# Strassen's scheme for the second mixture's first product, in pairs of token tiles

## The chip, the cores and the metric

The kernel runs on one core of one Trainium2 chip. Its engines work beside each other, each through its own queue in order: PE multiplies matrices into PSUM, ACT and DVE work on tiles in SBUF and PSUM, POOL on tiles in SBUF, SP's queue issues most DMA transfers. The metric is the device time of one execution in microseconds, as the median of several runs.

## The reference

A memory attention feeds two mixtures. What the change touches is the second one, on 4608 tokens of 512 features:

```python
x = _moe_ref(x=x, **moe_kwargs)                 # 4608 x 512, from the first mixture
h = x @ w_in                                    # w_in 512 x 1024
h_max = np.max(h, axis=-1, keepdims=True)
e = np.exp(h - h_max)
sm = e / (np.sum(e, axis=-1, keepdims=True) + 1e-09)
solu = h * sm
mu = np.mean(solu, axis=-1, keepdims=True)
var = np.mean((solu - mu) ** 2, axis=-1, keepdims=True)
ln = (solu - mu) / np.sqrt(var + 1e-06) * g_ln
return (ln @ w_out).astype(np.float32)          # w_out 1024 x 512
```

## The kernel before

Attention and the first mixture go over eight batches, each in two halves (`n`, `j`). In a half, `gemm1` makes 2048 hidden features in eight pairs `fp` (24 matmuls of 288 columns each; ACT squares, DVE casts and subtracts), and `gemm2` four blocks `d` of the result (48 matmuls each). ACT scales each block, `absmax` takes its maximum on DVE, and SP stores it to DRAM (`x2_d`), in groups of 1152 tokens that share one power-of-two scale.

The second mixture works on 36 tiles of 128 tokens. Every operand of a product is kept as two float16 tiles, a high part (written by ACT) and the rest (a subtraction on DVE): `split`. A product then takes three passes: high by high, high by low, low by high. For tile `i`: `load_x` fetches it, `split_x` splits it, `gemm3` multiplies it with `w_in` (4 blocks of 128 features x 3 passes x 2 halves of 512 columns = 24 matmuls, into two PSUM banks). `solu_1` takes the row maximum out of PSUM (DVE) and Exp (ACT). `solu_2` multiplies the product with Exp and takes mean and variance (DVE), then POOL takes the power -1/2 and normalises. `solu_3` casts to the high half of `nat` (ACT), `solu_4` subtracts for its low half (DVE) and has SP transpose it by DMA to `lt`. `gemm4` multiplies `lt` with `w_out` (8 blocks x 3 passes = 24 matmuls of 512 columns), ACT scales the result, SP stores it.

The order on every engine is the order of the program (a manual schedule). In the last half of batch 7, PE's `gemm2` of blocks 1 to 3 alternates with `gemm3` of tiles 0 to 2; from there on `gemm3` of one tile alternates with `gemm4` of one three tiles back. The weights of the second mixture are split at `prep2`, steps 0 to 3, between blocks of `gemm2`. The maximum of the last group of tokens is taken by a matmul (`mm_max`).

Of the kernel before, what the change touches and what calls it, by code (L numbers as in the profile page):

```python
# [66 lines left out]
def tile_mem_attention__moe_relu2__solu_ln(  # L67
# [15 lines left out]
    nc = tc.nc  # L83
# [14 lines left out]
    NTILE = NT // 128  # L98
    scale = 1.0 / float(D) ** 0.5
# [21 lines left out]
    xsc = const.tile([128, NT // GRP], FP32)  # L121
    xiv = const.tile([128, NT // GRP], FP32)
# [968 lines left out]
    def gemm1(n, j):  # L1091
        if j == 0:
            cs, t = csc_t[n]
            nc.vector.tensor_scalar(out=cs, in0=iw, scalar1=t[:, 0:1], scalar2=None, op0=ALU.mult)
        for fp in range(KF // 2):
            gemm1_mm(n, j, fp)
            relu(j, fp)
            square(j, fp, "A")
            nc.vector.tensor_copy(  # L1099
                out=g_of(n, j, 0)[:, 2 * fp:2 * fp + 2, 0:BLK], in_=gt["r2", j, fp]  # L1100
            )
            square_lo(n, j, fp)
            if fp == 2 and j == 0:
                phi_sum(n + 1)

# [81 lines left out]
    def gemm2_mm(n, j, d, part=(0, 1)):  # L1187
# [5 lines left out]
        half = len(steps) // 2  # L1193
        for x in range(half * part[0], half * (part[-1] + 1)):
# [221 lines left out]
    def prep2_open():  # L1416
        attn_ctx.close()
        for nm, bufs in (("x", 3), ("s", 2), ("o", 2), ("m", 1)):
            pools_b[nm] = ctx.enter_context(tc.tile_pool(name=f"pb_{nm}", bufs=bufs))
        W2["t"] = wts.tile([128, 2, KD * DFF2 + KF2 * DM], FP16, tag="win", name="w2_t")  # L1420
        for i in range(8):
            tag = ("e2", "so", "nat", "lt")[i // 2]
            W2[i] = pools_b["s"].tile([128, 2, 512], FP32, tag=tag, name="w2", bufs=4 if tag == "lt" else 2)
            nc.sync.dma_start(out=flat(W2[i]), in_=w2_d[i])
        pools_b["ones"] = pools_b["m"].tile([128, 128], FP32, tag="ones", name="ones_m")
        nc.gpsimd.memset(pools_b["ones"], 1.0)

    def prep2_scale(nm):
        mx = st.tile([128, 1], FP32, tag="wmx", name="wmx", bufs=1)
        word_value(pk_t.pop(("m", nm)), mx)  # L1430
        if nm == "in":
            wsc = st.tile([128, 1], FP32, tag="w2sc", name="w2sc", bufs=1)
            nc.vector.tensor_copy(out=wsc, in_=pow2_scale(mx, iw2, "wsc"))
# [7 lines left out]
    def prep2_split(i):  # L1441
        nm, x = P2[i]
        if nm == "in":
            dst = W2["t"][:, :, x * DFF2:(x + 1) * DFF2]
            split(dst[:, 0], dst[:, 1], W2[i].rearrange("p a f -> p (a f)"), pk_t["s", nm])
        else:
            for a in range(2):
                kk = 2 * x + a
                dst = W2["t"][:, :, KD * DFF2 + kk * DM:KD * DFF2 + (kk + 1) * DM]
                split(dst[:, 0], dst[:, 1], W2[i][:, a], sgl[:, kk:kk + 1])  # L1450
# [8 lines left out]
    PREP2 = (  # L1459
        ((0, 1), ()), ((2, 3), ()), ((4, 5), ()), ((6, 7), (0,)), ((), (1,)), ((), (2,)), ((), ()), ((), ()),  # L1460
    )

    def prep2(i):
        sp, tiles = PREP2[i]
        if i == 2:
            for x in range(3):
                load_x(x)
        for x in sp:
            prep2_split(x)
        for x in tiles:  # L1470
            split_x(x)
            load_x(x + 3)
# [20 lines left out]
    def x_scale(g):  # L1493
        sc = pow2_scale(xal_t.pop(g), xiv[:, g:g + 1])
        nc.vector.tensor_copy(out=xsc[:, g:g + 1], in_=sc)
        nc.vector.tensor_tensor(out=xiv[:, g:g + 1], in0=xiv[:, g:g + 1], in1=iw2, op=ALU.mult)

    def split_x(i):
        if i >= NTILE:
            return  # L1500
        g = i * 128 // GRP
        if g in xal_t:
            x_scale(g)
        t = xt_t.pop(i)
        xs = pools_b["x"].tile([128, 2, KD, 128], FP16, tag="xs", name="xs")
        split(xs[:, 0], xs[:, 1], t, xsc[:, g:g + 1])
        xs_t[i] = (xs, xiv[:, g:g + 1])

    def gemm3(i):
        xs, iv = xs_t.pop(i)  # L1510
        wt = W2["t"][:, :, 0:KD * DFF2].rearrange("p a (k f) -> p a k f", k=KD)
        hp = ps_h.tile([128, 2, 512], FP32, tag="h", name="hp2")
        for kk in range(KD):
            for px, pws in ((0, (0, 1)), (1, (0,))):
                for pw in pws:
                    for a in range(2):
                        nc.tensor.matmul(  # L1517
                            out=hp[:, a, :],
                            lhsT=xs[:, px, kk, :],
                            rhs=wt[:, pw, kk, a * 512:(a + 1) * 512],  # L1520
                            start=(kk == 0 and px == 0 and pw == 0),
                            stop=(kk == KD - 1 and px == 1),
                        )
        return hp, iv
# [3 lines left out]
    def solu_1(i, hp, iv):  # L1528
        hv = hp.rearrange("p a f -> p (a f)")
        mx = st.tile([128, 1], FP32, tag="hmx", name="hmx")  # L1530
        nc.vector.tensor_reduce(out=mx, in_=hv, op=ALU.max, axis=AX)  # L1531
        nm = st.tile([128, 1], FP32, tag="nm", name="nm")
        nc.vector.tensor_scalar(out=nm, in0=mx, scalar1=iv[:, 0:1], scalar2=-1.0, op0=ALU.mult, op1=ALU.mult)  # L1533
        split_x(i + 3)
        load_x(i + 6)
# [3 lines left out]
            out=e, in_=hv, func=ACTF.Exp, scale=iv[:, 0:1], bias=nm[:, 0:1], accum_out=sm  # L1539
        )  # L1540
        so_t[i] = hv, iv, e, sm

    def solu_2(i):
        hv, iv, e, sm = so_t[i]
# [20 lines left out]
        so_t[i] = so  # L1565

    def solu_3(i):
        so = so_t[i]
        nat = pools_b["s"].tile([128, 2, DFF2], FP16, tag="nat", name="nat")
        nc.scalar.copy(out=nat[:, 0, :], in_=so)  # L1570
        so_t[i] = so, nat

    def solu_4(i):
        so, nat = so_t.pop(i)
        nc.vector.tensor_tensor(out=nat[:, 1, :], in0=so, in1=nat[:, 0, :], op=ALU.subtract)  # L1575
# [4 lines left out]
        ln_t[i] = lt  # L1580
# [12 lines left out]
    def gemm4(i):  # L1593
        lt = ln_t.pop(i)
        wt = W2["t"][:, :, KD * DFF2:].rearrange("p a (k f) -> p a k f", k=KF2)
        y = ps_y.tile([128, 512], FP32, tag="y", name="y2")
        steps = [(f, pl, pw) for f in range(KF2) for pl, pw in PASSES]
        for x, (f, pl, pw) in enumerate(steps):
# [3 lines left out]
                rhs=wt[:, pw, f, :],  # L1602
                start=(x == 0),
                stop=(x == len(steps) - 1),
            )
        o = pools_b["o"].tile([128, DM], FP32, tag="o", name="o")
        nc.scalar.activation(out=o, in_=y[:, 0:DM], func=ACTF.Copy, scale=io2[:, 0:1])  # L1607
        for x, (off, n, bb, c, p) in enumerate(runs(i * 128, 128)):
            eng = nc.scalar if i == NTILE - 1 and x else nc.sync
            eng.dma_start(out=out_v[bb, c, p:p + n, :], in_=o[off:off + n, :])  # L1610

# [50 lines left out]
    with tc.manual_schedule():  # L1662
# [16 lines left out]
        def tile_mm(i):  # L1679
            h3_t[i] = gemm3(i)  # L1680

        def tile_rest(i):


            solu_1(i, *h3_t.pop(i))
            if i:
                solu_3(i - 1)
            if i == NTILE - 1:
                solu_4(i - 1)
            solu_2(i)  # L1690
            if i and i != NTILE - 1:
                solu_4(i - 1)

        h3_t = {}
        LAST = NB - 1
        for n in range(1, NB):
            for j in range(2):
# [7 lines left out]
                for d in range(KD):  # L1705
# [66 lines left out]
```

## Time and profile before

| | us |
|---|---|
| median of 3 runs | 1079.24 |
| lowest and highest | 1078.04, 1079.5 |
| the profiled execution, its time | 1078.8 |
| the profiled execution, its span from first to last instruction | 1077.0 |

The profile is one execution. An engine's busy share is an average over the whole span; the kernel has stages of quite different make-up, so stages are read by stretches of time. In the stage of the second mixture PE alternates between `gemm3` (line 1517) and `gemm4` (line 1599), from 687 us to the end.

### The profile page before, as it was taken

How to read it: one execution, taken by the hardware profiler on the slowest of the kernel's cores; microseconds unless marked ns; L12 is line 12 of the kernel's file. 1: busy time of each engine (PE TensorE's matmuls, PEld its weight loads, DVE VectorE, ACT ScalarE, POOL GpSimd, SP SyncE). 2: the span in 40 equal slices, each digit the busy share in tenths (PEclk: the TensorE clock that was granted, in tenths of full speed). 3: DMA queues.
4: the chain of work that ended last, by engine and by line, in shares of the span. 5: the costliest groups of instructions: out<-in, count | busy, mean ns of one | idle time of the engine just before them, and what ended most of it. 6: DMA issues, size and time to landing. Idle time of an engine off the chain costs nothing.

```text
span 1077.0 us, 21231 instructions
## 1 busy us (share of the span) xinstructions
PE 1053.2 (98%) x8679; PEld 694.4 (64%) x8679; DVE 767.3 (71%) x1469; ACT 525.8 (49%) x775; POOL 174.1 (16%) x157
## 2 busy tenths in 40 slices
PE   5799999999999999999999999999999999999998
PEld 4577777777777777777777777754444444444443
DVE  4799988877777777777776866467666766666662
ACT  3689755663663663563664566332333333333322
POOL 0000200220120120120120100023223232232320
PEclk9999999999999999999999999999999999999999
DMA  9993534734734635635624142124343343443324
GB/s 303 268 269 128 127 109 93 173 90 101 173 91 112 162 91 117 156 92 129 144 91 106 37 175 62 41 73 115 89 115 100 100 108 88 108 106 100 88 59 108
DMA packets 204849, 129.25 MB, mean 120 GB/s; under 512 B 137424, under 2 KB 187856, under 8 KB 204752
## 3 DMA queue, kind: packets, MB, share of 16 engines
q1 hardware_dynamic: 204608, 127.70, 45.4%
q8 instruction: 68, 1.11, 0.5%
q14 instruction: 29, 0.24, 0.1%
q10 hardware_dynamic: 112, 0.20, 0.1%
q0 software_dynamic: 32, 0.00, 0.0%
HBM read 71.83 MB, written 23.07 MB: 88 GB/s over the span
## 4 chain that ended last, share of the span: by engine, by line
PE 96%; DMA 2%; DVE 1%; SPq 0%; issue 0%; ACT 0%; ACTq 0%
PE y L1196 33%; PE y L1599 17%; PE hp L1517 17%; PE hp L1114 15%; PE hp L1010 3%; PE y L1038 3%; DMA q_s<-in_q_dram 2%; PE wp L734 2%; PE sp L883 1%; PE kp L524 1%; PE wp L692 1%; DMA wt_s<-in_v_dram 1%; PE kp L564 1%; PE tq L644 0%; SPq L383 0%; PE kp L538 0%
## 5 line engine op out<-in xcount | busy, mean ns | idle before, releaser
L1196 PE MATMUL y<-g,w_out 128*128 128x288 f16 x2688 | 338.6, 286 | 0.0
L1196 PEld LDWEIGHTS <-w_out 128*128 128x128 f16 x2880 | 277.2, 97 | 86.5 <-issue 12.0
L1517 PE MATMUL hp<-w_t,xs 128*128 128x512 f16 x864 | 192.0, 379 | 0.0
L1599 PE MATMUL y<-w_t,lt 128*128 128x512 f16 x864 | 191.7, 379 | 0.0
L1114 PE MATMUL hp<-aT,vwt 128*128 128x288 f16 x1344 | 166.9, 286 | 0.0
L1114 PEld LDWEIGHTS <-vwt 128*128 128x128 f16 x1344 | 131.4, 98 | 33.2
L1599 PEld LDWEIGHTS <-lt 128*128 128x128 f16 x864 | 84.5, 98 | 101.7
L1517 PEld LDWEIGHTS <-xs 128*128 128x128 f16 x864 | 84.5, 98 | 101.4
L1561 POOL TENSOR_TENSOR rstd<-ve,nhalf 128x1 f32<-128x1 f32 x36 | 52.7, 1464 | 332.6 <-DVE mv L1559 332.6
L1531 DVE TENSOR_REDUCE hmx<-hp 128x1 f32<-128x1024 f32 x36 | 44.1, 1224 | 84.1 <-PE hp L1517 84.1
L322 ACT ACTIVATE xs<-xt,xsc 128x512 f16<-128x512 f32 x36 | 26.0, 721 | 151.3 <-PE hp L1517 129.9
L1213 ACT ACTIVATE x<-y,bcol,cs 128x288 f32<-128x288 f32 x60 | 35.2, 586 | 111.1 <-PE y L1196 96.2
L1179 DVE TENSOR_TENSOR g<-r_s,g 128x576 f16<-128x576 f32 x112 | 85.6, 764 | 3.8
L1172 ACT ACTIVATE r_s<-r 128x576 f32<-128x576 f32 x112 | 76.6, 684 | 17.5 <-DVE g L1179 14.3
L1125 ACT ACTIVATE r<-hp 128x576 f32<-128x576 f32 x120 | 77.5, 646 | 13.9 <-PE hp L1114 6.9
L319 DVE TENSOR_REDUCE xmx<-x 128x1 f32<-128x288 f32 x64 | 28.8, 450 | 53.6 <-ACT x L1213 53.3
L1099 DVE CAST g<-r_s 128x576 f16<-128x576 f32 x112 | 51.7, 462 | 21.3 <-ACT r_s L1172 21.3
L1538 ACT ACTIVATE e<-hp,nm,xiv 128x1024 f32<-128x1024 f32 x36 | 43.3, 1203 | 45.5 <-DVE nm L1533 45.5
L1607 ACT ACTIVATE o<-y,io 128x512 f32<-128x512 f32 x36 | 24.7, 687 | 53.0 <-issue 40.5
L1575 DVE TENSOR_TENSOR nat<-so,nat 128x1024 f16<-128x1024 f32 x36 | 43.8, 1216 | 5.4 <-ACT nat L1570 5.4
L1554 DVE BATCH_NORM_STATS2 bs<-so 128x6 f32<-128x512 f32 x72 | 46.3, 685 | 1.2
L1549 DVE SCALAR_TENSOR_TENSOR so<-hp,sm,e 128x1024 f32<-128x1024 f32 x36 | 46.2, 1284 | 1.3
(256 smaller groups left out, 1187.9 us busy)
## 6 DMA issues: line engine op xcount, KB each, us to landing
x_d<-x SPq DMA_DIRECT2D x64, 144.0 KB, 2.0
xt<-x_d SPq DMA_DIRECT2D x36, 256.0 KB, 3.1
kv_s<-in_k_dram SPq DMA_DIRECT2D x31, 288.0 KB, 8.2
kv_s<-in_v_dram SPq DMA_DIRECT2D x31, 288.0 KB, 8.8
q_s<-in_q_dram SPq DMA_DIRECT2D x21, 288.0 KB, 4.9
out_dram<-o SPq DMA_DIRECT2D x23, 192.0 KB, 2.6
w_out<-in_moe_w_in_dram SPq DMA_DIRECT2D x4, 1024.0 KB, 18.1
raw<-in_moe_w_out_dram SPq DMA_DIRECT2D x4, 1024.0 KB, 11.4
```

What stands on the lines that cost most here:

```text
L1099: nc.vector.tensor_copy(out=g_of(n, j, 0)[:, 2 * fp:2 * fp + 2, 0:BLK], in_=gt["r2", j, fp])
L1114: nc.tensor.matmul(out=hp[:, u, 0:BLK], lhsT=vt[:, pw, R, f * 128:(f + 1) * 128], rhs=aT[:, CJ * j:CJ * (j + 1), pa, R, :], start=(x == 0) ...
L1125: nc.scalar.activation(out=r, in_=gt.pop(("h", j, fp))[:, :, 0:BLK], func=ACTF.Relu, scale=scale)
L1172: nc.scalar.activation(out=r2, in_=r, func=ACTF.Square)
L1179: (nc.vector if eng == "D" else nc.gpsimd).tensor_tensor(out=g_of(n, j, 1)[:, fs, 0:BLK], in0=gt.pop(("r2", j, fp)), in1=g_of(n, j, 0)[:, ...
L1196: nc.tensor.matmul(out=y[:, 0:w], lhsT=w_out_t[d][:, pw, f, :], rhs=g_of(n, j, pg)[:, f, 0:w], start=(x == 0), stop=(x == len(steps) - 1),)
L1517: nc.tensor.matmul(out=hp[:, a, :], lhsT=xs[:, px, kk, :], rhs=wt[:, pw, kk, a * 512:(a + 1) * 512], start=(kk == 0 and px == 0 and pw == ...
L1531: nc.vector.tensor_reduce(out=mx, in_=hv, op=ALU.max, axis=AX)
L1549: nc.vector.scalar_tensor_tensor(out=so, in0=hv, scalar=sm[:, 0:1], in1=e, op0=ALU.mult, op1=ALU.mult)
L1554: nc.vector.bn_stats(out=bs[:, a, :], in_=so[:, a * 512:(a + 1) * 512])
L1561: nc.gpsimd.tensor_tensor(out=rstd, in0=ve, in1=nhalf, op=ALU.pow)
L1599: nc.tensor.matmul(out=y[:, 0:DM], lhsT=lt[:, pl, f, :], rhs=wt[:, pw, f, :], start=(x == 0), stop=(x == len(steps) - 1),)
```

## The change

The product with `w_in` is made for pairs of tiles by the Strassen scheme in Winograd's form. The pair's x is a 2 x 2 array of blocks (two token tiles, two halves of 256 features), `w_in` another (two halves of features, two halves of 512 columns). Eight block products become seven, of sums and differences. The four sums of x blocks are made on POOL (`sums_x`), those of `w_in` once, also on POOL (`w2_sums`). A block product is 6 matmuls of 512 columns. Each pair has three PSUM banks, two sets of them; what was read from PSUM by the steps that follow is now put together in an SBUF tile `so` of float32: ACT copies a bank (four copies to a pair), products are added on in the bank, and DVE adds two more banks to what was copied (`h_add`, three to a pair). Maximum, Exp and `solu_2` then read SBUF.

`pair` writes out the order of one pair's steps together with the rest of the pair before. `gemm4` is cut into quarters of 6 matmuls that stand between the block products (`fill`); in pairs 0 and 1 quarters of `gemm2` of blocks 1 to 3 of the last half take these places. Splits of x go in two parts. `prep2` is laid out anew: steps 5 and 7 stand in `gemm1` of the last half, and the split of `w_out` (`prep2_out`) stands in pair 0. The maximum of the last group is taken by POOL's all-reduce. Scales change by powers of two.

```diff
     def gemm1(n, j):
...
+            if n == NB - 1 and j:
+                prep2(4 + fp)
...
+    def gemm2_q(n, j, d, part):
+        gemm2_mm(n, j, d, (part,), 4)
+        if part == 3:
+            gemm2_out(n, j, d)
...
+    def w2_sums(k):
+        b11, b12 = W2[k][:, 0], W2[k][:, 1]
+        b21, b22 = W2[2 + k][:, 0], W2[2 + k][:, 1]
+        t = [pools_b["x"].tile([128, 2, 512], FP32, tag="xt", name="w2s") for x in range(2)]
+        for out_, x, y in ((t[0][:, 0], b12, b11), (t[0][:, 1], b22, t[0][:, 0]), (t[1][:, 0], b22, b12),
+                           (t[1][:, 1], b21, t[0][:, 1])):
+            nc.gpsimd.tensor_tensor(out=out_, in0=x, in1=y, op=ALU.subtract)
+        W2["sum", k] = t
...
     def prep2(i):
...
+        if i == 0:
+            w2_sums(0)
+            for k in range(2):
+                w2_split(k, 0)
+                w2_split(k, 1)
+        elif i == 1:
+            w2_split(0, 2)
+            w2_split(0, 3)
+            w2_sums(1)
+        elif i == 2:
+            w2_split(1, 2)
+            w2_split(1, 3)
+            load_x(0)
+            load_x(1)
+        elif i == 3:
+            sums_x(0)
+            x_col(0)
+        elif i == 5:
+            split_part(0, 0)
+        elif i == 7:
+            split_part(0, 1)
+            load_x(2)
+            sums_x(1)
...
+    def sums_x(p):
...
+        a11, a12, a21, a22 = x_blocks(p)
+        sm = pools_b["x"].tile([128, 4, 2, 128], FP32, tag="xm", name="xm", bufs=1)
+        for x, in0, in1, op in (
+            (0, a21, a22, ALU.add), (1, sm[:, 0], a11, ALU.subtract),
+            (2, a11, a21, ALU.subtract), (3, a12, sm[:, 1], ALU.subtract),
+        ):
+            nc.gpsimd.tensor_tensor(out=sm[:, x], in0=in0, in1=in1, op=op)
...
+    def split_part(p, part):
...
+        parts = ((slice(3, 7), xt_t["m", p]),) if part == 0 else (
+            (slice(0, 2), t[:, :, 0:128].rearrange("p (b k) t -> p b k t", b=2)),
+             (slice(2, 3), t[:, 2:4, 128:256].unsqueeze(1)),
+        )
+        for b, src in parts:
+            nc.scalar.activation(out=xs[:, 0, b], in_=src, func=ACTF.Copy, scale=sc)
+        for b, src in parts:
+            nc.vector.scalar_tensor_tensor(
+                out=xs[:, 1, b], in0=src, scalar=sc, in1=xs[:, 0, b], op0=ALU.mult, op1=ALU.subtract
+            )
...
+    PROD = {1: (0, 0, 0), 2: (2, 1, 1), 5: (1, 3, 3), 6: (0, 4, 4), 3: (1, 6, 2), 7: (0, 5, 5), 4: (0, 2, 6)}
+
+    def product(p, i):
+        xs = xs_t[p][0]
+        bank, a, b = PROD[i]
+        first = i in (1, 2, 5)
+        steps = [(kk, px, pw) for kk in range(2) for px, pws in ((0, (0, 1)), (1, (0,))) for pw in pws]
+        for x, (kk, px, pw) in enumerate(steps):
+            nc.tensor.matmul(
+                out=hp_t[p][bank],
+                lhsT=xs[:, px, a, kk, :],
+                rhs=W2["lo"][kk][:, b, :] if pw else W2["hi"][:, b, kk, :],
...
+    def h_add(out_, bank):
+        nc.vector.tensor_tensor(out=out_, in0=bank, in1=out_, op=ALU.add)
+
+    def pair(p, fill, at=(2, 1, 1, 3)):
...
+        for i in (1, 2, 5):
+            product(p, i)
+        if p:
+            solu_max(q, 1)
+        split_part(p + 1, 0)
+        out4(2 * p - 5)
+        nc.scalar.copy(out=ha[:, 0:512], in_=bx)
+        if p:
+            solu_exp(q, 1)
+        h_add(ha[:, 0:512], bz)
+        fills(at[0])
+        if p:
+            solu_2(q, 1)
+            solu_3(q, 0)
+        nc.scalar.copy(out=hb[:, 512:1024], in_=by)
+        if p:
+            solu_4(q, 0)
+        split_part(p + 1, 1)
+        load_x(p + 3)
+        if p == 0:
+            for x in range(4):
+                prep2_out(x)
+        product(p, 6)
+        fills(at[1])
+        product(p, 3)
+        nc.scalar.copy(out=ha[:, 512:1024], in_=bx)
+        if p:
+            solu_3(q, 1)
+        sums_x(p + 2)
+        fills(at[2])
+        h_add(ha[:, 512:1024], by)
+        solu_max(p, 0)
+        product(p, 7)
+        out4(2 * p - 4)
+        solu_exp(p, 0)
+        h_add(hb[:, 512:1024], bx)
+        if p:
+            solu_4(q, 1)
+        fills(at[3])
+        solu_2(p, 0)
+        product(p, 4)
+        nc.scalar.copy(out=hb[:, 0:512], in_=bx)
+        fills(8)
...
+        pair(0, [lambda d=d, x=x: gemm2_q(LAST, 1, d, x) for d in (1, 2) for x in range(4)])
+        pair(1, [lambda x=x: gemm2_q(LAST, 1, 3, x) for x in range(4)], (0, 1, 1, 2))
+        x_max(3)
+        xal_t[3] = all_max(xal_t[3], "xal")
+        for p in range(2, NPAIR):
+            pair(p, tiles4(p - 2))
+        p = NPAIR - 1
+        rest = tiles4(p - 1) + tiles4(p)
+        solu_max(p, 1)
+        out4(2 * p - 3)
+        solu_exp(p, 1)
+        solu_2(p, 1)
+        solu_3(p, 0)
+        solu_4(p, 0)
+        for x, f in enumerate(rest):
+            f()
+            if x == 2:
+                solu_3(p, 1)
+                solu_4(p, 1)
```

In `pair`, `q` is the pair before, `ha` and `hb` are the two tiles' rows of `so`, and `bx`, `by`, `bz` the three banks.

## Rows read from the trace of the kernel before

**Rows 1.** The page's table of engines: busy us (share of the span), instructions.

```profile
PE 1053.2 (98%) x8679; PEld 694.4 (64%) x8679; DVE 767.3 (71%) x1469; ACT 525.8 (49%) x775; POOL 174.1 (16%) x157
```

**Rows 2.** Stretches of time: busy us of each engine, PE clock, DMA share, GB/s.

```profile
640.00:690.00 50.00, 50.00 (x399) 38.64 (x398) 28.11 (x47) 26.71 (x40) 0.00 (x0) 1.00 0.20 65
...
900.00:1000.00 100.00, 100.00 (x465) 45.33 (x464) 65.09 (x130) 33.57 (x47) 27.13 (x20) 1.00 0.40 101
```

**Rows 3.** The chain that ended last: start us, us, what.

```profile
675.67 11.85 PE y L1196 x96
...
1036.28 10.36 PE hp L1517 x48
1046.64 25.91 PE y L1599 x120
```

**Rows 4.** Groups of instructions: shapes, count, busy us, mean ns, idle before.

```profile
L222 PE MATMUL mp<-dg,ones_m 128*128 128x128 f32 x2 | 0.4, 274 | 0.0
...
L325 DVE SCALAR_TENSOR_TENSOR w_t<-w,w2sc,w_t 128x1024 f16<-128x1024 f32 x4 | 5.0, 1279 | 0.6 <-ACT w_t L322 0.6
...
L900 DVE TENSOR_TENSOR e<-sp,e 96x512 f32<-96x512 f32 x21 | 14.3, 681 | 0.5
...
L960 POOL TENSOR_TENSOR e<-e,ssm 96x512 f32<-96x512 f32 x18 | 18.8, 1046 | 153.6 <-DVE ssm L955 108.9 <-DMA kv_s<-in_v_dram 44.7
L481 POOL TENSOR_TENSOR phi_sb<-phi_sb,pm 128x1152 f32<-128x1152 f32 x5 | 13.1, 2619 | 0.0
```

**Rows 5.** Timeline of DVE in one steady tile: start us, us, instruction.

```profile
865.38 1.23 DVE L1531 TENSOR_REDUCE hmx<-hp 128x1 f32<-128x1024 f32 x1 [2.66 <-PE hp L1517]
...
866.77 0.74 DVE L325 SCALAR_TENSOR_TENSOR xs<-xt,xsc,xs 128x512 f16<-128x512 f32 x1
...
868.27 0.15 DVE L1545 TENSOR_SCALAR sm<-sm 128x1 f32<-128x1 f32 x1 [0.76 <-ACT e L1538]
...
871.87 1.22 DVE L1575 TENSOR_TENSOR nat<-so,nat 128x1024 f16<-128x1024 f32 x1
```

**Rows 6.** Groups of the stretch from 720 to 1040 us.

```profile
L1517 PEld LDWEIGHTS <-xs 128*128 128x128 f16 x739 | 72.3, 98 | 87.2
...
L1607 ACT ACTIVATE o<-y,io 128x512 f32<-128x512 f32 x31 | 21.3, 687 | 39.0 <-issue 37.0 <-PE y L1599 1.4 <-ACT nat L1570 0.6
```

**Rows 7.** DMA issues from 720 us on: count, KB each, median us to landing.

```profile
xt<-x_d SPq DMA_DIRECT2D x27, 256.0 KB, 3.1
...
lt<-nat SPq DMA_TRANSPOSE x35, 3.7
```

**Rows 8.** Line 1561 (ns min/median/max), then timeline where POOL and DVE meet.

```profile
L1561 POOL TENSOR_TENSOR rstd<-ve,nhalf x36: 549/1515/1546, 699.3 to 1057.8; 128x1 f32<-128x1 f32 x36
...
871.98 1.52 POOL L1561 TENSOR_TENSOR rstd<-ve,nhalf 128x1 f32<-128x1 f32 x1 [7.55 <-DVE mv L1559]
...
1049.15 1.22 DVE L1531 TENSOR_REDUCE hmx<-hp 128x1 f32<-128x1024 f32 x1
...
1049.74 1.20 POOL L1562 TENSOR_SCALAR so<-so,mv,rstd 128x1024 f32<-128x1024 f32 x1
...
194.88 1.16 POOL L469 PARTITION_ALL_REDUCE pm<-pmx  x1
...
195.12 1.06 DVE L1179 TENSOR_TENSOR g<-r_s,g 128x576 f16<-128x576 f32 x1
```

**Rows 9.** Timeline of one feature pair of gemm1 in the last half.

```profile
671.22 0.46 DVE L1099 CAST g<-r_s 128x576 f16<-128x576 f32 x1 [0.21 <-ACT r_s L1172]
671.29 0.65 ACT L1125 ACTIVATE r<-hp 128x576 f32<-128x576 f32 x1
671.72 0.76 DVE L1179 TENSOR_TENSOR g<-r_s,g 128x576 f16<-128x576 f32 x1
671.98 0.68 ACT L1172 ACTIVATE r_s<-r 128x576 f32<-128x576 f32 x1
```

More of the change, by code (lines that the diff above doesn't have):

```diff
@@ L1192, in gemm2_mm @@
         steps = [(f, pw, pg) for f in range(KF) for pw, pg in PASSES]
-        half = len(steps) // 2
-        for x in range(half * part[0], half * (part[-1] + 1)):
+        q = len(steps) // of
+        for x in range(q * part[0], q * (part[-1] + 1)):
             f, pw, pg = steps[x]
@@ L1439, in prep2_scale, with w2_split, prep2_out @@
         pk_t["s", nm] = wsc
[L1441 to L1450, printed above, removed]
+    def w2_sums(k):
[6 more added lines that the diff above has]
+        W2["sum", k] = t
+    def w2_split(k, part):
+        b = (slice(0, 1), slice(1, 3), slice(3, 5), slice(5, 7))[part]
+        src = W2["sum", k][part - 2] if part > 1 else W2[2 + k] if part else W2[k][:, 0:1]
+        split(W2["hi"][:, b, k, :], W2["lo"][k][:, b, :], src, pk_t["s", "in"])
+    def prep2_out(i):
+        for a in range(2):
+            kk = 2 * i + a
+            split(W2["out"][:, 0, kk, :], W2["out"][:, 1, kk, :], W2[4 + i][:, a], sgl[:, kk:kk + 1])
     EARLY = {8 * n + i: u for u, (n, i) in enumerate(
@@ L1509, in gemm3 @@
[L1509 to L1524, printed above, removed]
@@ new lines, in split_x, with hidden_open @@
+    def split_x(p):
+        split_part(p, 0)
+        split_part(p, 1)
+    hp_t = {}
+    def hidden_open(p):
+        if p == 0:
+            hid_ctx.close()
+            pools_b["h"] = ctx.enter_context(tc.tile_pool(name="pb_h", bufs=2, space=PSUM))
+        hp_t[p] = [pools_b["h"].tile([128, 512], FP32, tag=f"h{x}", name="hb") for x in range(3)]
+    PROD = {1: (0, 0, 0), 2: (2, 1, 1), 5: (1, 3, 3), 6: (0, 4, 4), 3: (1, 6, 2), 7: (0, 5, 5), 4: (0, 2, 6)}
[9 more added lines that the diff above has]
+                rhs=W2["lo"][kk][:, b, :] if pw else W2["hi"][:, b, kk, :],
+                start=first and x == 0,
+                stop=x == len(steps) - 1,
+                skip_group_check=not first,
+            )
@@ L1591, in tile_mem_attention__moe_relu2__solu_ln, with gemm4 @@
     out_v = out.rearrange("(b p c) d -> b c p d", b=NB, c=C)
[L1593 to L1596, printed above, removed]
+    def gemm4(i, part):
+        if part == 0:
+            gt["y4", i] = ps_y.tile([128, 512], FP32, tag="y", name="y2")
+        lt, y = ln_t[i], gt["y4", i]
         steps = [(f, pl, pw) for f in range(KF2) for pl, pw in PASSES]
[L1598 removed]
+        for x in range(6 * part, 6 * part + 6):
+            f, pl, pw = steps[x]
             nc.tensor.matmul(
@@ L1610, in gemm4, with tiles4 @@
             eng.dma_start(out=out_v[bb, c, p:p + n, :], in_=o[off:off + n, :])
+    def tiles4(p):
+        return [lambda i=i, part=part: gemm4(i, part) for i in (2 * p, 2 * p + 1) for part in range(4)]
     def load_sb():
```

201 lines of the change are left out of this document (104 added, 97 removed).

## The prediction

> **What bounds the kernel now.** I read the page's table of engines first: PE is busy 98% of the span, no other engine more than 71% [rows 1]. An average over stages can mislead, so next came the stretches: from 640 us on PE is busy in every microsecond, at full granted clock; in the steady pairs DVE is busy 65%, ACT 34%, POOL 27% [rows 2]. The chain of waits says the same of the end: gemm3's last 48 matmuls stand in it for 10.36 us, then gemm4's last 120 for 25.91 us, with nothing between [rows 3]. One 512-column matmul thus costs 10.36/48 = 0.2158 us, whichever product it belongs to, and a pair of tiles takes 2 x 48 of them, 20.72 us. In this stage a matmul less is 0.2158 us less, as long as no other engine needs more than PE's new time per pair. That condition is the whole prediction.
>
> **What is taken away.** Each of the 18 pairs had 2 x 24 matmuls in gemm3; seven products of six make 42. 108 matmuls x 0.2158 = **-23.3 us**, and a pair's slot becomes 90 x 0.2158 = 19.42 us. Replacing the column maximum of the last group by POOL's all-reduce takes two f32 matmuls of 0.274 us off PE [rows 4], **-0.5 us**; an all-reduce stood 1.16 us on POOL elsewhere [rows 8], once.
>
> **What is added, by engine and pair.** DVE before, per tile [rows 5]: maximum and nm 1.39 us (865.38 to 866.77), split 0.74, solu_2 3.60 (868.27 to 871.87), subtraction for nat 1.22; 6.95 us, 13.9 per pair. After: those without the splits 12.42; the splits cover seven blocks of 256 columns for four, in pieces of 1024, 512 and 256 columns: 1.28 [rows 4], 0.74 [rows 5] and by the slope between these some 0.48, 2.5 together; three h_add of 512 columns, PSUM with SBUF, nearest row 0.68 [rows 4], 2.04. **17.0 us of the 19.42**, 87%. ACT: 34% of 20.72 is 7.0 us before [rows 2]; four more copies out of PSUM at 0.69, the row of o [rows 6], and 768 more columns of splits at the same rate, 1.0, give 10.8 us: no bound. POOL: per tile the power and the normalising pass, 0.55 (its shortest) and 1.20 us [rows 8]; per pair 3.5, and four subtractions of 256 columns; 512 columns took 1.05 and 1152 took 2.62 [rows 4], so some 0.56 each, 5.7 us together.
>
> **Does PE wait inside a pair?** Time from the pair's first product, in units of six matmuls (1.295 us): products 1, 2 and 5 end at 1.3, 2.6 and 3.9; two quarters of gemm4; product 6 starts at 6.5, product 3 at 9.1, product 7 at 11.7, product 4 at 16.8. Each of these four adds to a PSUM bank that has to be read first. Product 6 needs ACT's copy of product 1: ACT has a split and an output copy before it and ends it at 2.2. Product 3 needs the copy of product 5, behind Exp and one nat copy: 5.4. Product 7 needs the copy after product 6 (ends 7.8): 8.7. Product 4 needs DVE's h_add after product 7 (ends 13.0). DVE's queue, by the durations above: the maximum of the last tile to 1.1, split to 2.4, h_add after product 2 to 3.4, solu_2 after Exp (3.6) to 7.2, nat to 8.5, split to 9.7, h_add when product 3 has ended (10.4) to 11.2, maximum to 12.6, h_add after product 7 to 13.8; product 4 has 3 us to spare. After it nat to 15.0 and solu_2 to 18.6, 0.8 us ahead of the next pair. ACT's Exp, nat copies and POOL's pass lie beside this and end before DVE asks for them. Each buffer of x (two, loaded by SP after DVE's last split) has a whole slot to land: 256 KB took 3.1 us [rows 7]; SP has the same transposes and output stores per pair, and one load for two. The two pairs whose tokens lie in two scale groups cost DVE two more column operations; the scale's own were there before. So by durations alone a steady pair is PE's.
>
> **The lock.** The power on POOL took 0.55 us at best but 1.5 us in most cases [rows 8]: it comes while DVE subtracts two SBUF tiles into nat and ends 0.4 us after that. Once it is DVE that waits: beside POOL's all-reduce (194.88 to 196.04) DVE's subtraction of two SBUF tiles took 1.06 for 0.76 us [rows 8, 9]. But a DVE instruction with one operand in PSUM ran beside POOL's pass, both at full speed (1.22 and 1.20 us) [rows 8]. So what counts is DVE's two-SBUF instructions beside POOL's. The change makes more of both: the Exp product now has both operands in SBUF, and POOL gets the sums. Laid on the queue above: the power wants to start at 7.3 in nat's stretch, the normalising pass follows and meets the second split (at 8.5), the sums mostly fall beside h_add and maximum, which have at most one SBUF operand. If POOL goes first each time, the split loses 0.4 + 1.15 us and the first split of the next pair up to 0.5: 19.05 us by this count. If DVE goes first, 0.8 us is lost: 17.8 us. Which order the chip takes no row shows, but both fit in 19.42, and the waits for products 3 and 7 in DVE's queue shrink by what is lost before them. So **0** for the 16 steady pairs; bounds 0 and, if every POOL microsecond held DVE, (17.0 + 5.7 - 19.42) x 18 = 59 us, which the queue above speaks against.
>
> The Trainium skill's page "SBUF — State Buffer", section "Who interferes with whom", states this as a rule: a VectorE instruction with two SBUF inputs and a GpSimd instruction that reads SBUF exclude each other for the whole instruction, whichever starts first. The rows above agree with it. Applied without the order of the queues, all of POOL's 5.7 us would count, and the sum would come out slower; that is the third rival below.
>
> **Before the steady pairs.** The sums of w_in run on POOL beside gemm1's last block, the splits of pair 0 go to ACT and DVE between its second half's feature pairs. There ACT needs 1.33 us (relu and square) of PE's 1.47 per feature pair, DVE 1.22 [rows 9]; split_part adds, by the row of o, about 1.1 us to ACT at the second and 1.3 at the fourth. With three PSUM buffers relu may be some 2.3 us late; I get the relu of the fifth at 9.95 us after the block's start, needed at 10.3. POOL's sums can hold DVE's subtraction. **+0.5 us**, between 0 and 2. prep2_out (eight splits of 512 columns, 5.9 us on DVE [rows 5], about as much on ACT) moves into pair 0, whose slot is 9.1 + 8 x 1.48 (gemm2's 11.85 us for 96 matmuls [rows 3], twelve to a quarter) = 20.9 us; DVE there has no previous pair's tile, so it fits. Pair 1 has only four quarters: 15.0 us for 17.0 of DVE and two row maxima. DVE falls some 2.9 us behind, plus its lock; product 4 of pairs 1 and 2 waits for h_add, and behind it on PE the last quarter and the next pair. **+1.3 us**, between 0 (no lock; the spare 3 us at product 4 cover it) and 4.
>
> **The tail.** After the last product PE has nine quarters of gemm4, 11.65 us, before it needs tile 34. Until then: copy 0.9, maximum 1.39, Exp 1.4, solu_2 3.60, nat 1.22, transpose 3.7 us to landing [rows 7], 12.2, with four hand-overs at 0.1 some 12.5. **+0.9 us**, between 0 and 2.5. Tile 35 follows 4 us later, under gemm4 of 34.
>
> Sum: -23.3 - 0.5 + 0 + 0.5 + 1.3 + 0.9 = **-21.1 us**. The profiled execution: span 1077.0, time 1078.8; with the change span 1055.9, time 1057.7. The median of the runs is 0.44 above the profiled time (the table of times): **1058.1 us**.
>
> **Rivals.** *DVE sets the pair.* 87% before any lock leaves 2.4 us; hand-overs and a lock that costs more than I laid out may need them. At 20.0 us per pair: 16 steady pairs x 0.58 = 9.3 us more, 1067; between 1063 and 1076. For it: the held POOL instructions [rows 8]; against: most of POOL's work falls beside PSUM operands. *No gain that can be measured*: DVE's period happens at 20.6 to 20.8, 1077 to 1081.4. *Slower:* POOL holds DVE in more than 20.72 - 17.0 = 3.7 of its 5.7 us per pair; from there DVE's period is above the old slot. At 4.6 us: 21.6 us, 18 x 0.9 = 16 over before, with the tail some 1096. Against it: the sums are queued behind the pass and meet the maximum, which reads one tile. *The products save nothing* because six-matmul groups in changing banks are slower: loads of weights took 98 ns under 216 [rows 6], one for each matmul before too, and gemm2 changes banks without a gap [rows 3]; no chance of its own.
>
> **Chances.** PE sets the pair, as forecast: 0.70, own range 1055.4 to 1063. DVE sets it but below the old slot: 0.20. Within 0.2% (2.2 us, about what a measurement of this kernel tells from no change): 0.03. Slower: 0.07. Faster 0.90. The range goes from 1055.4 (the full -23.8 us) to 1070 and leaves out the upper half of the second case and the two last.
>
> **What the changed kernel would show.** 756 product matmuls at an unchanged pitch; steady pairs of 19.4 us; DVE near 87% in the steady pairs; idle PE before product 4 in pairs 1 and 2 alone, and about 1 us before gemm4 of tile 34; the normalising pass and the second split lengthened where they meet. Wrong if product 4 waits for h_add in every pair, or if product 7 waits for ACT's copy, which I give 3 us.

## Result and profile after

| | before | after |
|---|---|---|
| median of the runs compared, us | 1078.64 (1078.04 to 1079.5, 4 runs) | 1064.82 (1064.4 to 1068.53, 4 runs) |
| the profiled execution, time / span | 1078.8 / 1077.0 | 1064.4 / 1062.6 |

The ratio is 0.9879, with a 95% interval from 0.9855 to 0.9902: faster, by 13.8 us between the medians. The forecast was 1058.1 us, 6.7 lower. In the spans: 21.1 us were forecast, 14.4 came.

The page of the changed kernel, engines as in [rows 1]:

```profile
PE 1031.9 (97%) x8569; PEld 684.2 (64%) x8569; DVE 831.4 (78%) x1548; ACT 579.5 (55%) x869; POOL 232.8 (22%) x237
```

PE has 110 instructions less: 108 matmuls of the product and the two of the maximum. DVE, ACT and POOL all have more to do, as the prediction's ledger said. Next the stretches, with the columns of [rows 2] (us, busy us of PE, PEld, DVE, ACT, POOL, clock, DMA share, GB/s):

```profile
720.00:740.00 20.00, 20.00 (x94) 9.11 (x93) 13.28 (x25) 6.59 (x10) 6.40 (x8) 1.00 0.22 54
740.00:760.00 20.00, 13.67 (x53) 5.56 (x51) 17.40 (x39) 10.06 (x17) 8.96 (x10) 0.83 0.40 93
760.00:780.00 20.00, 20.00 (x94) 9.06 (x93) 17.41 (x34) 10.26 (x17) 8.68 (x9) 1.00 0.51 131
784.29:803.71 19.42, 19.42 (x91) 8.82 (x90) 16.21 (x31) 10.12 (x16) 7.59 (x9) 1.00 0.43 109
880.00:920.00 40.00, 40.00 (x187) 18.18 (x186) 34.05 (x64) 20.83 (x31) 15.85 (x18) 1.00 0.42 106
```

One stretch stands out: from 740 to 760 us PE lacks 6.3 us and its granted clock is 0.83. On both sides PE is full, and a steady pair (784.29 to 803.71) is 19.42 us long. PE's waits from 640 us to the end (what waited, for whom: us in total, times, the longest) show the same:

```profile
PE hb L1610 <- ACT so L1701: 6.3, 1, 6.3
PE y L1760 <- DMA lt<-nat: 0.5, 1, 0.5
```

So in this whole stage PE waits twice, once for 6.3 us. The chain that ended last, at that place and in a steady pair, with the columns of [rows 3]:

```profile
749.17 2.72 PE hb L1610 x6
751.89 2.56 PE y L1760 x6
754.45 1.35 PE hb L1610 x6
755.80 1.29 PE y L1760 x6
...
784.29 3.88 PE hb L1610 x18
...
803.71 3.88 PE hb L1610 x18
```

The first twelve matmuls after the wait took 2.72 and 2.56 us per six where six take 1.29: the lower of the clock's two levels (1.2 for 2.4 GHz), 2.7 us more. The account of the spans: -23.3 (products), -0.5 (the two matmuls), +6.3 and +2.7 (this place), +0.5 (tile 34 at the end) = -14.3, where -14.4 was measured. What has to be explained is one stop of 9.0 us.

### The profile page after: what moved, and what is told of

The parts are those of the page before. It is cut to its first block, busy times and chain, and to the rows that moved or that the text cites. A ratio compares the mean times of both kernels' runs of the same rounds, so it can differ in the third digit from the quotient of the medians.

```text
span 1062.6 us, 21249 instructions
## 1 busy us (share of the span) xinstructions
PE 1031.9 (97%) x8569; PEld 684.2 (64%) x8569; DVE 831.4 (78%) x1548; ACT 579.5 (55%) x869; POOL 232.8 (22%) x237
## 4 chain that ended last, share of the span: by engine, by line
PE 87%; DVE 6%; DMA 3%; issue 2%; ACT 1%; SPq 0%; POOL 0%; ACTq 0%; DVEq 0%; POOLq 0%
PE y L1200 32%; PE hp L1118 15%; PE y L1760 15%; PE hb L1610 13%; PE y L1040 2%; PE hp L1012 2%; PE wp L736 2%; DMA q_s<-in_q_dram 2%; PE sp L885 1%; PE kp L526 1%; DMA wt_s<-in_v_dram 1%; DVE hmx L1629 1%; DMA kv_s<-in_v_dram 1%; DVE bs L1654 1%; DVE so L1649 1%
## 5 line engine op out<-in xcount | busy, mean ns | idle before, releaser
L1760 PE MATMUL y<-w_t,lt 128*128 128x512 f16 x864 | 201.0, 381 | 0.5 <-DMA lt<-nat 0.5
L1610 PE MATMUL hb<-w_t,xs 128*128 128x512 f16 x504 | 165.3, 381 | 6.3 <-ACT so L1701 6.3
L1610 PEld LDWEIGHTS <-xs 128*128 128x128 f16 x756 | 74.3, 98 | 95.0 <-issue 8.4
L1610 PE MATMUL hb<-w_lo,xs 128*128 128x512 f16 x252 | 96.0, 381 | 0.0
L1661 POOL TENSOR_TENSOR rstd<-ve,nhalf 128x1 f32<-128x1 f32 x36 | 35.3, 982 | 215.2 <-DVE mv L1659 208.3
L1668 ACT CAST nat<-so 128x1024 f16<-128x1024 f32 x36 | 37.4, 1040 | 53.9 <-POOL so L1662 53.9
L1681 DVE TENSOR_TENSOR so<-hb,so 128x512 f32<-128x512 f32 x54 | 37.2, 689 | 27.4 <-PE hb L1610 27.2
L962 POOL TENSOR_TENSOR e<-e,ssm 96x512 f32<-96x512 f32 x18 | 18.8, 1046 | 153.8 <-DVE ssm L957 121.1
L1638 ACT ACTIVATE e<-so,nm,xiv 128x1024 f32<-128x1024 f32 x36 | 44.7, 1242 | 9.9 <-DVE nm L1631 9.9
L1662 POOL TENSOR_SCALAR so<-so,mv,rstd 128x1024 f32<-128x1024 f32 x36 | 49.0, 1361 | 3.8
```

Of the source, the lines that this page charges most:

```text
L1610: nc.tensor.matmul(out=hp_t[p][bank], lhsT=xs[:, px, a, kk, :], rhs=W2["lo"][kk][:, b, :] if pw else W2["hi"][:, b, kk, :], start=first an ...
L1638: nc.scalar.activation(out=e, in_=h_of(p, t), func=ACTF.Exp, scale=iv[:, 0:1], bias=nm[:, 0:1], accum_out=sm)
L1662: nc.gpsimd.tensor_scalar(out=so, in0=so, scalar1=mv[:, 0:1], scalar2=rstd[:, 0:1], op0=ALU.add, op1=ALU.mult)
L1668: nc.scalar.copy(out=nat[:, 0, :], in_=h_of(p, t))
L1760: nc.tensor.matmul(out=y[:, 0:DM], lhsT=lt[:, pl, f, :], rhs=W2["out"][:, pw, f, :], start=(x == 0), stop=(x == len(steps) - 1),)
```

## Where the stop comes from

The stop is in pair 3, at product 6, which adds to a bank that ACT must copy first (line 1701). POOL just before it, in the changed kernel (start us, us, instruction, idle before and who ended it):

```profile
721.02 1.20 POOL L1662 TENSOR_SCALAR so<-so,mv,rstd 128x1024 f32<-128x1024 f32 x1
728.29 0.56 POOL L184 PARTITION_ALL_REDUCE al<-xmax  x1 [6.07 <-DVE mv L1659]
735.73 0.59 POOL L1661 TENSOR_TENSOR rstd<-ve,nhalf 128x1 f32<-128x1 f32 x1 [6.88 <-issue]
```

Between a normalising pass and the next power POOL does a single thing, the all-reduce that the change put behind pair 1, and stands still for 6.07 us before it and 6.88 us behind it. The DVE instruction named as releaser had ended before the pass began; it ended no wait. Two lines of the source, with a queue's own instruction that the timeline doesn't count as busy (ns min/median/max, first and last start), say more:

```profile
L184 POOLq MODIFY_POOL_CONFIG  x8: 7/12/15, 230.3 to 722.5; - x8
```

```profile
L1661 POOLq MODIFY_POOL_CONFIG  x2: 82/82/83, 728.8 to 728.8; - x2
```

A MODIFY_POOL_CONFIG stands at 722.5, right behind the pass, and another at 728.8, right behind the all-reduce, this one for line 1661, an ordinary operation. After each comes the standstill. The Trainium skill's page "GPSIMD Engine Reference", section "2.1 Instruction dispatch", says that the first call of a freshly loaded routine pays a load of code of about 6 us; the trace agrees with its 6.07 us. The 6.88 us behind the all-reduce are read from the trace alone.

What was queued behind it, on ACT and DVE of the changed kernel, in order of time:

```profile
737.66 1.05 ACT L1668 CAST nat<-so 128x1024 f16<-128x1024 f32 x1 [11.52 <-POOL so L1662]
...
739.19 1.23 ACT L1638 ACTIVATE e<-so,nm,xiv 128x1024 f32<-128x1024 f32 x1
...
744.55 1.21 DVE L1629 TENSOR_REDUCE hmx<-so 128x1 f32<-128x1024 f32 x1
...
746.74 0.15 DVE L1545 TENSOR_TENSOR xiv<-xiv 128x1 f32<-128x1 f32 x1
746.92 1.15 ACT L1580 ACTIVATE xs<-xm,xsc 128x1024 f16<-128x1024 f32 x1 [5.93 <-DVE xiv L1545]
...
748.54 0.57 ACT L1701 COPY so<-hb 128x512 f32<-128x512 f32 x1
...
749.17 0.59 PE L1610 MATMUL hb<-w_t,xs 128*128 128x512 f16 x1 [6.33 <-ACT so L1701]
```

ACT's queue is in order: the cast waits 11.52 us for POOL's pass, Exp of the next tile stands behind the cast, DVE's `solu_2` needs Exp, and the next maximum stands behind `solu_2` in DVE's queue. Behind that maximum stand the column operations of pair 4, whose tokens lie in two scale groups (lines 238 to 1545, to 746.89). ACT's split of pair 4 waits 5.93 us for them, and behind the split stands the copy that PE wants. The copy would have been due at 742.84, when PE ran out of work.

Theory A: the all-reduce's standstill on POOL's queue makes the stop by itself. Its rival: other work is late there, above all the backlog that the prediction expected of the short pair 1, and the all-reduce only stands beside it. When the first experiments had shown that A alone isn't enough, two forms of it were set against each other: C, the standstill hurts where the column operations follow it, so that moving these away is enough; D, it hurts where DVE comes out of the short pair 1 with a backlog.

## Experiments

**The maximum without POOL.** The changed kernel with the last group's maximum taken by a matmul in front of pair 4:

```diff
-        xal_t[3] = all_max(xal_t[3], "xal")
+        dg = xp.tile([128, BLK], FP32, tag="x2", name="dg")
+        nc.vector.memset(dg[:, 128:256], 1.0)
+        nc.vector.tensor_scalar(out=dg[:, 0:128], in0=ident, scalar1=xal_t[3], scalar2=None, op0=ALU.mult)
         for p in range(2, NPAIR):
+            if p == 4:
+                mp = ps_y.tile([128, 512], FP32, tag="y", name="mp")
+                nc.tensor.matmul(out=mp[:, 0:128], lhsT=dg[:, 128:256], rhs=dg[:, 0:128], start=True, stop=True)
+                xal_t[3] = st.tile([128, 1], FP32, tag="xal", name="al")
+                nc.vector.tensor_reduce(out=xal_t[3], in_=mp[:, 0:128], op=ALU.max, axis=AX)
```

> The changed kernel with the last group's maximum taken by a matmul of ones again (one f32 matmul in front of pair 4), in place of POOL's all-reduce. Theory A: POOL stands still for about 6 us ahead of an all-reduce and 7 us behind it (722.2 to 728.3 and 728.9 to 735.7 in the changed kernel's trace), so the normalising of pair 1 comes late, PE idles 6.3 us and then runs 2.7 us longer at half clock; without it 8 to 9 us come back, some 1056 us, no idle PE between 740 and 750 us, granted clock 1.000. Theory B: DVE's backlog after pair 1's short slot makes PE wait before pair 3; then the idle stays and the gain is under 1 us.

Measured: 1054.86 us (1054.06 to 1057.09), ratio to before 0.9789 [0.977, 0.9808]. PE waits once from 640 us on, for the transpose of tile 34 (0.6 us). This version beats both kernels: some 10 us under the changed one, 23.5 under the one before. The rival alone is out, since pair 1 is as short here.

**The same all-reduce later.** Moved behind pair 7, in steady running:

```diff
-        xal_t[3] = all_max(xal_t[3], "xal")
         for p in range(2, NPAIR):
+            if p == 8:
+                xal_t[3] = all_max(xal_t[3], "xal")
```

> The changed kernel with the all-reduce moved from behind pair 1 to behind pair 7, in the steady pairs. Theory A: the same two standstills of POOL there, the same loss at the new place, 1064 to 1065 us, within 2 us of the changed kernel. Theory B: in the steady pairs DVE has no backlog, so the idle PE of 740 to 750 us goes and little of it comes back, 1056 to 1058 us.

Measured: 1055.05 us (1053.5 to 1055.32), 0.9784 [0.9763, 0.9805], slightly under what B gave. Its POOL timeline:

```profile
832.62 1.19 POOL L1662 TENSOR_SCALAR so<-so,mv,rstd 128x1024 f32<-128x1024 f32 x1
839.57 0.51 POOL L184 PARTITION_ALL_REDUCE al<-xmax  x1 [5.76 <-issue]
847.15 0.59 POOL L1661 TENSOR_TENSOR rstd<-ve,nhalf 128x1 f32<-128x1 f32 x1 [7.07 <-DVE so L1681]
```

The standstill is there, as long as before, and PE doesn't wait. So theory A falls too: 13 us of standing POOL cost nothing here. The difference is what is late already. Here the next power comes 14.4 us after its pair's start (832.80), in the changed kernel 19.0 (pair 2 starts at 716.77). In the pair after, ACT's copy for product 6 ends 3.6 us before PE wants it, where the changed kernel has it 6.3 us late.

**The same all-reduce in the old kernel.** Before, with `all_max` for the matmul, behind a tile:

```diff
-                xal_t[3] = mm_max_put(xal_t[3])
-            if i == 9:
-                xal_t[3] = mm_max(xal_t[3])
+                xal_t[3] = all_max(xal_t[3], "xal")
```

> The kernel before with that one edit alone: its last group's maximum by POOL's all-reduce, behind tile 5, in place of the matmul. Theory A: POOL stands still for about 13 us, but it was idle 7.5 us of each tile's 10.4, and the old order has gemm4 three tiles behind; a loss between 0 and 6 us, less than in the changed kernel. Theory B: no loss, 1078 us, and no standstill.

Measured: 1077.65 us (1076.34 to 1078.72), 0.9999 [0.999, 1.0008], no PE idle. POOL stands for 6.19 us before the all-reduce at 755.80 and 6.94 behind it, and nothing that PE needs comes late by it.

**Eight products.** An eighth block product of six matmuls per pair, which nobody reads:

```diff
+        product(p, 8)
```

> The changed kernel with an eighth block product of six matmuls in each pair behind the seventh product (product 2 once more, into its own bank after that has been read; nothing reads the result). If PE alone sets the steady pairs: 20.72 us per pair, 18 x 1.295 = 23.3 us over the changed kernel less what the longer slots give back around pairs 1 and 2, 1083 to 1088 us. If DVE or the lock set them: less than half of that.

One run: 1087.35 us, 22.5 over the changed kernel, where 18 x 1.295 = 23.3 stands for the matmuls alone; a steady pair goes from 790.38 to 811.10, 20.72 us. PE alone sets the steady pairs; the stop stays (5.6 us).

**The column operations early.** The all-reduce left behind pair 1; the columns of pair 4 made in `prep2`, step 3, and kept:

```diff
+            x_col(4)
...
     def x_col(p):
+        if p in xcol_t:
+            return xcol_t[p]
...
+        xcol_t[p] = c
```

> The changed kernel, all-reduce behind pair 1 as it was, but the scale columns of pair 4 (which straddles two groups) made early, beside prep2's step 3, so that ACT's split in pair 3 waits for nothing on DVE. Theory C: part of the loss is that ACT's split, with the copy for product 6 behind it, stands from 741.0 to 746.9 us for DVE's column operations, which are queued behind the maximum; then product 6 starts some 5 us earlier, the wait moves to product 3 (behind Exp of the late tile) and is 2 to 4 us; 1058 to 1062 us. If the column operations don't matter: 1064 to 1065.

Measured: 1059.32 us (1058.24 to 1062.49), 0.9842 [0.9822, 0.9861]. PE's waits:

```profile
PE hb L1614 <- ACT so L1713: 2.4, 1, 2.4
PE hb L1614 <- ACT so L1705: 1.2, 1, 1.2
```

The edit puts four lines in front, so line 1705 is the copy for product 6 and line 1713 the copy of product 5, for product 3. The stop at product 6 falls from 6.3 to 1.2 us; ACT's split now waits for POOL's sums of x, late as well. Another 2.4 us come at product 3, whose copy stands behind late Exp and `nat`. By the traces C has the larger part (9.0 us come down to 3.6), not the whole.

**Behind pair 6 and behind pair 2.** The two places that the theories tell apart: behind pair 6 the columns of group 2 follow, far from pair 1; behind pair 2 no columns follow at once, and the backlog is smaller. Edits as for the late all-reduce, with `p == 7` and `p == 3`.

> The changed kernel with the all-reduce behind pair 6: no backlog there, but pair 8 makes the scale of group 2 in front of its split, as pair 3 does in the changed kernel. Theory C (the standstill hurts where a split with column operations follows): some 3 us of idle PE before product 6 of pair 8, 1057 to 1061 us. Theory D (it hurts where DVE has a backlog from pair 1's short slot): no idle PE, 1054 to 1056 us.

> The changed kernel with the all-reduce behind pair 2: part of the backlog is there (POOL normalises the last tile some 3 us into the next pair, against 5.4 behind pair 1 and 0.8 behind pair 7), and no column operations follow in the pair after. Theory C alone: no idle PE, 1054 to 1056 us. Theory D alone: a loss between that behind pair 1 and none, 1057 to 1062 us. Both needed: 1054 to 1057 us.

Measured: behind pair 6, 1060.56 us (1058.94 to 1061.15), 0.9841 [0.9826, 0.9856]; behind pair 2, 1056.13 us (1054.99 to 1057.97), 0.9804 [0.9789, 0.9819]. PE's longest wait with the all-reduce behind pair 6, and then behind pair 2:

```profile
PE hb L1610 <- ACT so L1701: 3.1, 1, 3.1
```

```profile
PE hb L1610 <- ACT so L1709: 0.9, 1, 0.9
```

Far from pair 1's backlog the columns (of group 2, in front of pair 9's split) bring back the wait of the changed kernel, half as long and at the same product. The five versions with the all-reduce, with their ratios to before:

| short pair 1 just before | columns just behind | us | ratio |
|---|---|---|---|
| yes | yes (changed kernel) | 1064.8 | 0.9879 |
| no | yes (behind pair 6) | 1060.6 | 0.9841 |
| yes | no (early columns) | 1059.3 | 0.9842 |
| one pair later | no (behind pair 2) | 1056.1 | 0.9804 |
| no | no (behind pair 7) | 1055.1 | 0.9784 |

Without any all-reduce on POOL it is 1054.9 (0.9789). Neither C nor D alone fits: the standstill alone is covered in steady running, and each of the two other delays costs some 4 to 6 us, 10 together.

**How near DVE is to being the bound.** The version with the matmul, with three unread row maxima of 1024 columns more per pair on DVE, and with two:

```diff
+        for _ in range(3):
+            jk = st.tile([128, 1], FP32, tag="hmx", name="jk")
+            nc.vector.tensor_reduce(out=jk, in_=h_of(p, 0), op=ALU.max, axis=AX)
```

> The kernel with the matmul maximum, and in each pair three more row maxima on DVE behind the first tile's (1.25 us each, nothing reads them). The prediction's DVE need of 17.0 us per pair leaves 2.4 us: 3.75 us more make DVE the bound with 20.7 us per pair, 16 x 1.3 = 21 us more, 1072 to 1080 us, PE waiting for h_add at product 4 in each pair. If the lock makes DVE's need nearer 19 us: 45 to 55 us more. If DVE's need is under 15.7: no loss.

> The kernel with the matmul maximum, and in each pair two more row maxima on DVE (1.22 us each, nothing reads them). Three of them made a steady pair 20.4 us, so DVE's own need is 20.4 - 3 x 1.24 = 16.7 us; two more make 19.2, below PE's 19.43: steady pairs unchanged, a few us lost behind the short slot of pair 1 and in the tail, 1055 to 1060 us. If POOL's lock costs DVE more when less room is left: steady pairs above 19.43 and 1060 to 1070 us.

Three: 1081.8 us, one run, with pairs of 20.41 us ((1025.44 - 862.16)/8). Its PE waits, and one line of its chain:

```profile
PE hb L1610 <- DVE so L1681: 18.0, 15, 2.6
```

```profile
1025.44 3.46 DVE jk L1729 x3
```

Now product 4 waits for `h_add` in most pairs, and the three maxima stand in the chain with 3.46 us. DVE's own need is then about 20.41 - 3.46 = 16.95 us per pair, its waits for others included. The time is slightly over what was expected: the first pairs and the tail lose too. Two: 1062.7 us (1062.25 to 1063.56), 0.9861 [0.9845, 0.9877]; the steady pairs keep PE 99.4 to 99.6% busy, as expected, but the waits for `h_add` in five pairs, mostly from 690 to 760 us (5.0 us), and for the last transpose (1.8 us) put it 2.7 us above the expected range. Against the matmul version it loses 8 us, mostly in the first pairs and at the end.

**Less backlog.** The early columns, with the product with Exp left out for the tiles 1 and 2, of the pairs 0 and 1:

```diff
+        if (p, t) not in ((0, 1), (1, 0)):
             nc.vector.scalar_tensor_tensor(
                 out=so, in0=so, scalar=sm[:, 0:1], in1=e, op0=ALU.mult, op1=ALU.mult
             )
```

> The kernel with early columns (all-reduce behind pair 1), in which the product of tiles 1 and 2 with Exp is left out (two DVE instructions of 1.28 us in pair 1's part of the queue; the results of these two tiles are not the reference's). Theory D: what was left of the loss with early columns, some 4.5 us over the kernel with the matmul maximum, comes from DVE's backlog behind pair 1's short slot, which delays POOL's standstill; with 2.6 us less of it 1055 to 1057.5 us. If the rest has another cause: 1059 us as with early columns.

Measured: 1058.66 us (1056.66 to 1060.69), 0.9823 [0.9806, 0.9841]. In the trace PE's idle time falls from 3.6 to 2.4 us, towards D; in time the spread is wider than the 0.7 us between the two, and the measured time is not in D's range. The power came only some 1.3 us earlier against its pair, so little backlog was taken away, and in the profiled execution the lower clock behind the wait took back some 1.6 us (six matmuls in 2.56 us, the next six in 1.64).

**What the traces say together.** The times alone leave D open, and two things read in each trace settle more: when POOL's power behind the all-reduce starts, counted from the first product of its pair, and when ACT's copies for products 6 and 3 end, counted from the first product of the pair after. PE wants them at 6.5 and 9.1 us there, as long as it has not waited before.

| all-reduce | power starts, us | copy for 6 ends | copy for 3 ends | PE idle, us |
|---|---|---|---|---|
| behind pair 7 | 14.35 | 2.91 | 8.05 | 0 |
| behind pair 2 | 16.36 | 4.91 | 10.05 | 0.9 |
| behind pair 1, less backlog | 17.88 | 6.45 | 11.58 | 2.4 |
| behind pair 1, early columns | 19.19 | 7.75 | 12.88 | 1.2 + 2.4 |
| behind pair 6, columns follow | 15.93 | 9.71 | 12.36 | 3.1 |
| behind pair 1, columns follow (changed kernel) | 18.96 | 12.92 | 15.58 | 6.3 |

In the four without columns both copies move with the power one for one, and PE's idle time is, within 0.2 us, what they exceed its marks by. With columns the copy for product 6 ends some 5.3 us later against the power. The power's start is the standstill (13.0 to 13.9 us, behind pair 6 14.9) on top of how late POOL's last pass ends in the pair: 1.0 us behind pair 7, 3.3 behind pair 2, 5.4 behind pair 1, and 4.0 with less backlog. So C and D are two parts of one sum, and the last experiment followed D as far as it took backlog away: 1.3 us of lateness less, 1.2 us of idle PE less.

## Why the prediction was right and where it failed

*The steady pairs: right.* 756 product matmuls (504 and 252 in two groups of line 1610) at the old pitch, 12 pairs between 784.29 and 1017.39 of 19.42 us each. With eight products the pair is 20.72 again. "0 for the 16 steady pairs" holds for 15; the rival in which DVE sets the pair did not come.

*DVE's need: right.* 17.0 us were worked out. In the windows DVE is busy 16.21 of 19.42 and 34.05 of 40 us, 83 to 85% where 87 was said, and some 16.95 us by the experiment with three more maxima. In the steady pairs PE waited for nobody, and DVE waited for PE, as its group of `h_add` says from 765 to 1030 us:

```profile
L1681 DVE TENSOR_TENSOR so<-hb,so 128x512 f32<-128x512 f32 x41 | 28.3, 691 | 27.0 <-PE hb L1610 26.9
```

*The lock: cheaper than either order.* A steady pair of the changed kernel, where DVE's `nat` and second split meet POOL's power and pass:

```profile
791.18 1.22 DVE L1673 TENSOR_TENSOR nat<-so,nat 128x1024 f16<-128x1024 f32 x1
792.31 1.14 DVE L1582 SCALAR_TENSOR_TENSOR xs<-xt,xsc,xs 128x512 f16<-128x512 f32 x2
```

```profile
791.29 1.51 POOL L1661 TENSOR_TENSOR rstd<-ve,nhalf 128x1 f32<-128x1 f32 x1 [6.15 <-DVE mv L1659]
792.91 1.53 POOL L1662 TENSOR_SCALAR so<-so,mv,rstd 128x1024 f32<-128x1024 f32 x1
```

The power took 1.51 us as in [rows 8], the pass 1.53 for its 1.20, and DVE went from `nat` to the split with no gap and lost nothing. Where the two queue up here, POOL waited. The third rival, POOL holding DVE, did not come in the steady pairs. POOL's own work was put too low: 5.7 us were said, and it was busy 7.59 us in this pair, with sums of 0.72 us for 0.56 beside the lengthened power and pass. One row fits the prediction's rule less than it says: in [rows 8] the subtraction beside the all-reduce ended 0.14 us after it, where waiting for its end would have left the whole 0.76.

*The head:* +0.5 was said, no idle PE came from 640 us to the stop. The lock is there (below); what covered it no run shows.

*The transition: mis-sized, and by another mechanism.* +1.3 us was worked out from DVE's backlog, as waits of product 4 for `h_add` in pairs 1 and 2. PE did not wait there at all, so the spare time at product 4 covered the backlog. The 9.0 us came at product 6 of pair 3, for ACT's copy. The prediction's place (behind the short slot of pair 1) was right, and the backlog there is part of it, but as a cover that is missing when POOL stops.

The prediction had this hand-over on its list, with the copy done 2.2 us into the pair. In steady pairs that is so (2.1 us). It counted the column operations of a pair in two scale groups as DVE's time alone, though, and not as something that ACT's split stands for. In pair 3 of the version with the matmul, which starts at 734.53, the copy ends at 6.0 us, and of 4.3 us to spare 0.5 are left:

```profile
738.29 1.15 ACT L1580 ACTIVATE xs<-xm,xsc 128x1024 f16<-128x1024 f32 x1 [4.27 <-DVE xiv L1545]
...
739.92 0.57 ACT L1701 COPY so<-hb 128x512 f32<-128x512 f32 x1
...
741.00 0.38 PE L1610 MATMUL hb<-w_t,xs 128*128 128x512 f16 x1
```

*The failed step:* "Replacing the column maximum of the last group by POOL's all-reduce takes two f32 matmuls of 0.274 us off PE, -0.5 us; an all-reduce stood 1.16 us on POOL elsewhere [rows 8], once." It was costed by its own duration, without its queue. Its price on POOL is some 13 us, in which nothing behind it runs; in this place that is 9.0 us for 0.5 gained. The trace of before had it in rows that were not read as such, the waits of POOL, and the all-reduce of one of the groups:

```profile
POOL al L182 <- DVE g L1099: 18.1, 3, 6.2
```

```profile
236.74 0.59 POOL L182 PARTITION_ALL_REDUCE al<-xmax  x1 [6.08 <-DVE g L1099]
```

Three idle times of nearly the same length (5.78 to 6.22 us) ahead of three all-reduces are no wait for three different inputs. The half behind the all-reduce stood there too, after the one at 116.94, with a MODIFY_POOL_CONFIG of its line at 118.3 and a releaser that it does not read:

```profile
125.16 3.47 POOL L481 TENSOR_TENSOR phi_sb<-phi_sb,px 96x1536 f32<-96x1536 f32 x1 [6.86 <-DMA x_d<-x]
```

The reading was not free: the one at 236.74 got its input from DVE only at 235.63, and the one of [rows 8] ran with no gap beside it, between two copies of POOL. There the changes stood elsewhere: a MODIFY_POOL_CONFIG at 130.0 and the next at 196.7, right behind the second copy, both ahead of long idle times; in between POOL did only all-reduces and copies.

*The tail:* +0.9 was said, 0.5 came: after `lt` landed, 48 matmuls follow at once.

```profile
1043.98 3.63 DMA lt<-nat
...
1047.66 10.55 PE y L1760 x48
```

With the all-reduce priced rightly the other terms stand: -23.3 + 0.6 = -22.7, and the version with the matmul, which is that sum, came out 22.8 us under before by its ratio. The range held because it reached to 1070 for a rival that did not come, and that is luck: the loss that came was priced in none of its terms.

What stays open: in time, as against the traces, the part of the backlog is not shown, since the last experiment took too little of it away.

## What to carry to other kernels

Cost an instruction by what its queue does around it: before an instruction moves to an engine, look at the idle time ahead of and behind every instance of it in the trace, and take equal idle times with doubtful releasers as part of its price. Work out the spare time of a hand-over in the exceptional steps too, here in pair 3, where ACT's split waits for the columns on DVE. A long stop of an engine with slack is free only where nothing else is late, so put it in steady running and not behind a shortened step or ahead of work that all others wait for: the same all-reduce cost 10 us in one place and nothing six pairs later. One unread product, and a few unread reductions, tell which engine sets a loop and how much room the next one has.

## What the runs showed of the hardware that was not expected

An all-reduce among POOL's arithmetic stood between two standstills in all eight traces that have one in this stage: 5.71 to 6.44 us ahead of it and 6.79 to 7.43 behind it (6.07 and 6.88 in the changed kernel, 6.44 and 7.42 behind pair 6). Between copies of POOL (at 194.88 us, before) there was none.

POOL's sums of `w_in` beside `gemm1` held DVE's cast as well as its subtraction. The cast has one SBUF input, and the prediction had counted only instructions with two:

```profile
637.82 1.53 DVE L1101 CAST g<-r_s 128x576 f16<-128x576 f32 x1
639.38 1.70 DVE L1183 TENSOR_TENSOR g<-r_s,g 128x576 f16<-128x576 f32 x1
641.00 0.45 DVE L1101 CAST g<-r_s 128x576 f16<-128x576 f32 x1
```

The first two ran beside POOL's sums (635.75 to 640.47), the third alone: 1.53 for 0.45 us. The Trainium skill's page "SBUF — State Buffer", section "Who interferes with whom", counts copies and casts among what can contend with GpSimd, when their operands meet its conditions; the trace agrees.

After 6.3 us of idle PE the clock was at the lower of its levels for twelve matmuls. After 3.1 us (behind pair 6) it was not (granted 1.00); after one idle time of 2.4 us it was for a part of them in one run (0.91, less backlog) and not in another (1.00, early columns).
